# The first batch's slot pairs in three stages set apart in program order, and the filter's sign put in once

## The chip, the cores and the metric

The kernel runs on one core of one Trainium2 chip. A time is that of one execution in microseconds of device time; kernels are compared by the median of their runs. The profile is of one such execution.

## What is computed

Eight sequences of 3008 tokens with 256 channels go through a filter in the frequency domain and then through an MLP with an intermediate width of 2048. All inputs are float32 but for the MLP's weights, which arrive as float64.

```python
X = np.fft.rfft(x, axis=1)                    # x: 8 x 3008 x 256
Y = X * (filt_r + 1j * filt_i)[None]          # 1505 frequencies x 256
x = np.fft.irfft(Y, n=3008, axis=1).reshape(8 * 3008, 256)
h = x @ w_in                                  # 256 x 2048
out = (h / (1 + np.exp(-1.702 * h))) @ w_out  # 2048 x 256
```

## The kernel before

The length 3008 is 64 x 47. A forward transform is a DFT over 64 (tiles `s1`), a DFT over 47 (`s2`), the product with the filter, and the two inverse DFTs (`i2`, then `i1`). Real input leaves 32 slots of 48 rows and 256 channels; a step handles two slots, called a **pair** here, so a batch has 16 pairs. In a tile of a pair, rows 0 to 47 hold the real part and rows 64 to 111 the imaginary part (112 partitions, the 16 between are zero).

The first batch (`first_fft`) has nothing to run beside. Its six input tiles are multiplied by `t1_0` (L331) and copied to `a_t` (L334). Then for each pair g: TensorE (PE) transposes four 128x96 blocks (L342, tile `z`), ScalarE (ACT) copies them to SBUF (L344, `zs`), PE does the filter's DFT (L348, `s2`, printed as `s`), `product` multiplies by the filter on VectorE (DVE, L365 and L366) and GpSimd (POOL, L367), PE does the inverse DFT of the product (L354, `i2`, printed as `i`), and ACT copies the result into `b_t` (L355).

`product` is a complex multiplication. Some slots stand for the conjugate of a stored frequency, so the imaginary part of the filter has a sign of its own for each row and slot, in the table `sign`. Before, DVE put it in as a per-row scalar, in four operations of 48 rows x 256 channels for each pair, in every batch (L365).

Filter values are loaded by SyncE's DMA queue (SP) in two transfers of 192 KB for a pair, one for rows 0 to 47 and one for rows 64 to 111. In the first batch eight buffers `f_s` (made of `f_buf`, `f_y` and `f_o`) rotate, and loads run six pairs ahead.

The MLP's weights arrive as 64-bit values and are turned into pairs of float32 parts by ACT, DVE and POOL (`weights`, `weight`, L219 to L236). The generator `weights` has 20 steps: steps 0 to 3 only load a weight, step 4 loads the fifth and starts four conversions, and each later step starts one and finishes one. `run(w_parts, n)` runs n steps. After the first batch comes `mlp` for 48 tiles of up to 512 tokens (L515 to L529), and between its matmuls the transforms of later batches (`fft`) are spread; these use the same `product`, with `f_buf` loaded anew for each pair (L413).

The order of the instructions on an engine is set by a scheduler from the program's order. Instructions given to `keep_in_program_order` keep their order among themselves: among them are the loads of SP in the first part (`load_in`) and the first four ACT operations of `weight` (L219). Each engine, and the DMA queue of SP, takes its instructions in that order, so one that waits holds all behind it.

Of the kernel before, what the change touches and what calls it, by code (L numbers as in the profile page):

```python
# [9 lines left out]
F32 = mybir.dt.float32  # L10
# [19 lines left out]
def _tables():  # L30
# [65 lines left out]
    d_0[:96] = de[rows, 0:2]  # L96
    e_0 = de[:, 2:4, rows].reshape(P, 2, 2, 2, NH).transpose(0, 1, 4, 3, 2)
    sign = np.zeros((P, NS))
    sign[0:48], sign[64:Q] = _places()[3], -_places()[3]
    tabs = [t1_0, t1, t2, d_0, e_0, np.eye(P), sign, de]  # L100
    return np.concatenate([a.reshape(P, -1) for a in tabs], 1).astype(np.float32)

# [48 lines left out]
def tile_kernel(  # L151
# [145 lines left out]
    def first_fft():  # L297

        d_0 = table["d_0"].rearrange("p (m c) -> p m c", m=2)
        e_0 = table["e_0"].rearrange("p (m c) -> p m c", m=2)

        a_t = [const.tile([P, NS, 96], F32, tag=t, name=f"a_t{m}") for m, t in enumerate(("wi_1", "wo_1"))]
        f_s = [f_buf] + [sb.tile([Q, 4, 2, D], F32, tag="y", name=f"f_y{i}") for i in range(2)]
        f_s = [f[:, 2 * i : 2 * i + 2] for f in f_s for i in range(2)]
        f_s += [sb.tile([Q, 2, 2, D], F32, tag="out", name=f"f_o{i}") for i in range(2)]
        pin = tc.keep_in_program_order

        def load_f(g):  # L310
# [24 lines left out]
        yield
        for g in range(16):
            if 6 <= g + 6 < 16:
                load_f(g + 6)
            z_ps = bank(f"z_0_{g}")
            for u in range(2):  # L340
                for m in range(2):
                    nc.tensor.transpose(z_ps[:96, u, P * m : P * m + P], a_t[m][:, 2 * g + u], table["eye"])  # L342
            z = sb.tile([96, 2, D], F32, tag="half", name=f"zs_0_{g}", bufs=4)
            nc.scalar.copy(z, z_ps[:96])  # L344
            ps = bank(f"s2_0_{g}")
            ms = [(slice(0, 1), 1), (slice(1, 2), 0)] if g == 0 else [(slice(0, 2), 0)]
            for u, m in ms:
                nc.tensor.matmul(ps[:Q, u], d_0[:96, m], z[:, u], start=True, stop=True)  # L348
            u1 = c_buf[g % 3]
            product(g, ps, u1, f_s[g % 8])  # L350
            ps = bank(f"i2_0_{g}").rearrange("p a d -> p (a d)")[:, 0:384].rearrange("p (m u c) -> p m u c", m=2, u=2)
            for u in range(2):
                for m in range(2):
                    nc.tensor.matmul(ps[:, m, u], u1[:Q, u, P * m : P * m + P], e_0[:Q, int(g + u == 0)], start=True, stop=True)  # L354
            nc.scalar.copy(b_t[:, :, :, 2 * g : 2 * g + 2], ps.rearrange("p m u c -> p m c u"))  # L355
            yield

    def product(i, xs, u1, fr):

        u2 = u_buf[i % 2]  # L360
        f_r, f_i = fr[:, :, 0, :], fr[:, :, 1, :]
        for u in range(2):
            for h, o in ((slice(0, 48), slice(64, Q)), (slice(64, Q), slice(0, 48))):
                sg = sign[h, 2 * i + u : 2 * i + u + 1]
                nc.vector.scalar_tensor_tensor(u2[o, u], xs[h, u], sg, f_i[h, u], ALU.mult, ALU.mult)  # L365
        nc.vector.tensor_tensor(u1, xs[:Q], f_r, ALU.mult)  # L366
        nc.gpsimd.tensor_tensor(u1, u1, u2, ALU.add)  # L367

# [7 lines left out]
    def fft(b):  # L376
# [33 lines left out]

        def load_f(i):
            for k in range(2):
                load_in(f_buf[64 * k : 64 * k + 48, 2 * (i % 2) : 2 * (i % 2) + 2], filt[:, 2 * i : 2 * i + 2])  # L413

        def second(i, m, src, name):

# [212 lines left out]
```

## Time and profile before

| | |
|---|---|
| median of 3 runs | 2533.18 us (2532.65 to 2534.22) |
| profiled execution | 2531.02 us, of which its span is 2529.2 us |
| mean granted clock of PE | 0.974 |
| busy: PE, DVE, ACT, POOL | 2441.0, 1601.1, 1301.9, 831.3 us |

The span is the time from the first to the last instruction of the profile. In a row of the timeline stand the start, the busy time, the engine, line and operation, the output and input tiles, the shape, and in brackets the idle time before it and what ended that. In a row of groups stand the busy time, the mean of one in ns, and the idle time ahead of the group with what ended it. In a row of waits: who waited, for whom, us in total, how many times, and the longest.

### The profile page before, as it was taken

Reading aid. Unit: us, or ns where it says so; the run is one execution under the profiler, and the core shown is the slowest. Engines: PE = TensorE matmul, PEld = TensorE weight load, DVE = VectorE, ACT = ScalarE, POOL = GpSimd, SP = SyncE. Lnnn points to the kernel's source line nnn. Section 1 sums busy time; section 2 is a strip of 40 time slices with the busy share of each in tenths; the row PEclk is TensorE's granted clock in tenths of the full one; section 3 lists DMA queues with packets and bytes.
Section 4 is the critical chain, followed back from the end, with each engine's and each line's share of the span. In section 5 each row is a group of like instructions: output and inputs, shape, how many; then the busy total and the mean of one; then the engine's idle time right before and its main releaser. Section 6 shows DMA issues by size and latency. Waiting matters only on the chain.

```text
span 2529.2 us, 31965 instructions
## 1 busy us (share of the span) xinstructions
PE 2441.0 (97%) x11082; PEld 2005.1 (79%) x11082; DVE 1601.1 (63%) x2423; ACT 1301.9 (51%) x2409; POOL 831.3 (33%) x714
## 2 busy tenths in 40 slices
PE   7779999999999999999999999999999999999999
PEld 5457877887778888988877888888878888898887
DVE  4495788468845887378843887358863788432322
ACT  1265555555545555555554555555555565444443
POOL 2263454235422443244421454134432344100000
PEclk6589999999999999999999999999999999999999
DMA  6133543554445443454334343453434443300000
GB/s 180 44 100 108 117 110 85 133 133 111 107 113 137 102 103 92 133 121 98 92 104 123 97 103 81 127 129 96 110 84 134 102 105 93 72 15 9 17 9 17
DMA packets 139906, 243.48 MB, mean 96 GB/s; under 512 B 15328, under 2 KB 80992, under 8 KB 139744
## 3 DMA queue, kind: packets, MB, share of 16 engines
q1 hardware_dynamic: 61504, 130.58, 18.5%
q10 hardware_dynamic: 53152, 66.80, 10.0%
q0 software_dynamic: 25088, 44.05, 8.9%
q8 instruction: 88, 1.44, 0.2%
q14 instruction: 74, 0.61, 0.1%
HBM read 150.67 MB, written 90.70 MB: 95 GB/s over the span
## 4 chain that ended last, share of the span: by engine, by line
PE 73%; DMA 4%; DVE 3%; issue 1%; ACT 1%; SPq 0%; POOL 0%; ACTq 0%; POOLq 0%; DVEq 0%
PE o L529 32%; PE h L515 32%; PE i L486 3%; DMA br<-b_d 2%; PE s L423 2%; PE i L423 1%; DVE u_buf L365 1%; PE s L270 1%; PE s L269 1%; PE s L271 1%; DVE c_buf L374 1%; DVE gl L521 1%; DMA x<-in_x_dram 1%; DMA b_d<-b 1%; DMA zy<-a_d 1%
## 5 line engine op out<-in xcount | busy, mean ns | idle before, releaser
L515 PE MATMUL h<-y,wi 128*128 128x512 f32 (+1 forms) x4608 | 1173.8, 388 | 4.2 <-POOL wi L236 2.1
L521 DVE TENSOR_TENSOR gl<-g,gh 128x512 fp32r<-128x512 f32 (+1 forms) x768 | 650.0, 849 | 692.8 <-ACT gh L520 615.7
L515 PEld LDWEIGHTS h<-y,wi 128*128 128x128 f32 x4608 | 864.3, 189 | 178.4 <-POOL wi L236 3.3
L519 ACT ACTIVATE g<-h 128x512 f32<-128x512 f32 (+1 forms) x768 | 452.6, 589 | 917.7 <-PE h L515 802.8
L529 PE MATMUL o<-gh,wo 128*128 128x512 f32 (+1 forms) x3072 | 833.3, 390 | 15.6 <-ACT gh L520 11.6
L529 PEld LDWEIGHTS o<-gh,wo 128*128 128x128 f32 x3072 | 570.6, 189 | 137.4 <-ACT gh L520 18.3
L529 PE MATMUL o<-gl,wo 128*128 128x512 f32 (+1 forms) x1536 | 480.8, 389 | 11.7 <-DVE gl L521 11.4
L520 ACT ACTIVATE gh<-h 128x512 fp32r<-128x512 f32 (+1 forms) x768 | 448.4, 585 | 58.6 <-PE o L529 48.3
L438 POOL TENSOR_TENSOR zy<-c_buf,zy 48x512 fp32r<-48x512 f32 x224 | 335.4, 1497 | 93.2 <-DVE zy L437 81.9
L367 POOL TENSOR_TENSOR c_buf<-c_buf,u_buf 112x512 f32<-112x512 f32 x128 | 192.4, 1503 | 517.5 <-DVE c_buf L366 517.2
L529 PEld LDWEIGHTS o<-gl,wo 128*128 128x128 f32 x1536 | 284.6, 188 | 75.0 <-DVE gl L521 21.2
L387 POOL TENSOR_TENSOR xl<-x,xh 128x512 fp32r<-128x512 f32 x84 | 111.3, 1338 | 411.5 <-ACT xh L386 377.8
L365 DVE SCALAR_TENSOR_TENSOR u_buf<-c_buf,tab,f_buf 48x256 f32<-48x256 f32 x448 | 225.4, 542 | 6.6
L406 POOL DMA_DIRECT2D zy<-a_d x224 | 128.2, 575 | 285.9 <-PE s L423 102.4
L374 DVE TENSOR_TENSOR c_buf<-s,c_buf 48x512 f32<-48x512 f32 x224 | 154.2, 688 | 22.7 <-ACT c_buf L373 16.7
L374 DVE TENSOR_TENSOR b<-i,b 48x512 f32<-48x512 f32 x224 | 154.1, 688 | 8.8 <-ACT b L373 2.5
L373 ACT COPY c_buf<-s 48x512 f32<-48x512 f32 x224 | 130.1, 581 | 23.1 <-PE s L423 12.4
L373 ACT COPY b<-i 48x512 f32<-48x512 f32 x224 | 130.1, 581 | 16.6 <-DVE b L374 4.9
L437 DVE CAST zy<-c_buf 48x512 fp32r<-48x512 f32 x224 | 95.6, 427 | 56.9 <-POOL c_buf L367 52.9
L486 PEld LDWEIGHTS i<-tab,br 128*128 128x128 f32 x736 | 100.5, 195 | 26.8 <-issue 9.4
L486 PE MATMUL i<-tab,br 128*128 128x128 f32 x736 | 104.7, 280 | 13.6 <-DMA br<-b_d 9.6
L497 POOL CAST y<-carry 128x128 fp32r<-128x128 f32 x8 | 2.8, 375 | 261.0 <-PE h L515 260.8
(81 smaller groups left out, 1238.0 us busy)
## 6 DMA issues: line engine op xcount, KB each, us to landing
f_buf<-in_filt_dram SPq DMA_DIRECT2D x232, 192.0 KB, 3.2
zy<-a_d POOLq DMA_DIRECT2D x224, 192.0 KB, 3.6
x<-in_x_dram SPq DMA_DIRECT2D x48, 512.0 KB, 4.8
out_dram<-out SPq DMA_DIRECT2D x44, 512.0 KB, 3.4
a_d<-ah ACTq DMA_DIRECT2D x84, 256.0 KB, 3.5
a_d<-al ACTq DMA_DIRECT2D x84, 256.0 KB, 3.8
b_d<-b ACTq DMA_DIRECT2D x112, 192.0 KB, 2.6
br<-b_d SPq DMA_DIRECT2D x84, 256.0 KB, 4.6
```

The source lines that it names most:

```text
L365: nc.vector.scalar_tensor_tensor(u2[o, u], xs[h, u], sg, f_i[h, u], ALU.mult, ALU.mult)
L367: nc.gpsimd.tensor_tensor(u1, u1, u2, ALU.add)
L373: nc.scalar.copy(dst[h], ps[k][o])
L374: nc.vector.tensor_tensor(dst[h], ps[k][h], dst[h], ALU.add)
L406: nc.gpsimd.dma_start(zy[0][64 * k : 64 * k + 48, i % 2].rearrange("p k s d -> p k (s d)"), src.rearrange("n k s d -> n k (s d)"),)
L438: nc.gpsimd.tensor_tensor(y[o, k], u1[h], y[h, k].bitcast(F32), ALU.subtract)
L486: nc.tensor.matmul(ps[:, P * i : P * i + P], br[m][:, i], t2_sb, start=True, stop=True)
L515: nc.tensor.matmul(ps[:, :w], wi_sb[half][:, wk, kc, c], y[:, yk, kc, :w], start=n == 0, stop=n == 5)
L519: nc.scalar.activation(g[:, :w], ps[:, :w], AF.Gelu_apprx_sigmoid)
L520: nc.scalar.activation(gh[:, :w], ps[:, :w], AF.Gelu_apprx_sigmoid)
L521: nc.vector.tensor_tensor(gl[:, :w], g[:, :w], gh[:, :w].bitcast(F32), ALU.subtract)
L529: nc.tensor.matmul(pos[m][:, :w], wo[:, wk, P * m : P * m + P], gp[gk][:, :w], start=fc == 0 and n == 0, stop=fc == NFC - 1 and n == 2,)
```

## The change

1. The loop over the pairs of the first batch is cut into three functions. `turned(g)` is the transposes and their copy, `filtered(g)` the filter's DFT and the product, `inverse(g)` the inverse DFT and its copy. Step i of 19 runs `turned(i)`, `filtered(i - 1)` and `inverse(i - 3)`.
2. The sign is multiplied into the imaginary part of the filter by ACT, in two operations of 112x256 for each pair of the first batch, in `turned`. The signed rows 0 to 47 are stored to a DRAM buffer `fs` (192 KB for a pair, on SP's queue), and later batches load their filter from `fs`. The table `sign` now has the same sign in both halves.
3. `product` has two operations of 48x512 in place of four of 48x256: one with -1.0 as scalar, one plain multiplication.
4. Filter loads in the first batch run five steps ahead in place of six pairs.
5. The first eight steps of `weights` run after steps 2, 3, 5, 8, 13, 15, 17 and 19 of the first batch; before, four ran after steps 2, 5, 8 and 11 and four after the last pair.

```diff
-    sign[0:48], sign[64:Q] = _places()[3], -_places()[3]
+    sign[0:48] = sign[64:Q] = _places()[3]
...
+    fs = dram1.tile([48, NS, 2, D], F32, name="fs")
...
-        for g in range(16):
-            if 6 <= g + 6 < 16:
-                load_f(g + 6)
-            z_ps = bank(f"z_0_{g}")
+        def turned(g):
+            ps = bank(f"z_0_{g}")
...
+            zs[g] = sb.tile([96, 2, D], F32, tag="half", name=f"zs_0_{g}", bufs=4)
+            nc.scalar.copy(zs[g], ps[:96])
+            f = f_s[g % 8]
+            for u in range(2):
+                nc.scalar.activation(f[:, u, 1], f[:, u, 1], AF.Copy, scale=sign[:Q, 2 * g + u : 2 * g + u + 1])
+            load_in(fs[:, 2 * g : 2 * g + 2], f[0:48])
+
+        def filtered(g):
+            z = zs.pop(g)
...
+            product(g, ps, c_buf[g % 3], f_s[g % 8])
+
+        def inverse(g):
...
+        for i in range(19):
+            if 6 <= i + 5 < 16:
+                load_f(i + 5)
+            if i < 16:
+                turned(i)
+            if 1 <= i < 17:
+                filtered(i - 1)
+            if i >= 3:
+                inverse(i - 3)
             yield
...
-        for u in range(2):
-            for h, o in ((slice(0, 48), slice(64, Q)), (slice(64, Q), slice(0, 48))):
-                sg = sign[h, 2 * i + u : 2 * i + u + 1]
-                nc.vector.scalar_tensor_tensor(u2[o, u], xs[h, u], sg, f_i[h, u], ALU.mult, ALU.mult)
+        nc.vector.scalar_tensor_tensor(u2[0:48], xs[64:Q], -1.0, f_i[64:Q], ALU.mult, ALU.mult)
+        nc.vector.tensor_tensor(u2[64:Q], xs[0:48], f_i[0:48], ALU.mult)
...
-                load_in(f_buf[64 * k : 64 * k + 48, 2 * (i % 2) : 2 * (i % 2) + 2], filt[:, 2 * i : 2 * i + 2])
+                load_in(f_buf[64 * k : 64 * k + 48, 2 * (i % 2) : 2 * (i % 2) + 2], fs[:, 2 * i : 2 * i + 2])
...
-        if i in (2, 5, 8, 11):
+        if i in (2, 3, 5, 8, 13, 15, 17, 19):
             run(w_parts, 1)
-    run(w_parts, 4)
```

On the engines the order comes out as follows. PE, in the middle of the first batch, before (`z_5` is the transposed tile of pair 5, `s_0_4` the filter's DFT of pair 4, `i_0_3` the inverse of pair 3; the last number is the buffer's):

```order
L348 MATMUL s_0_4_303<-zs_4_301,tab 112x512
L354 MATMUL i_0_3_288<-tab,c_buf_78 128x96 x4
L342 MATMUL z_5_321<-tab,a_t_85 96x128
L342 MATMUL z_5_321<-tab,a_t_86 96x128
...
L354 MATMUL i_0_4_311<-tab,c_buf_79 128x96 x4
L348 MATMUL s_0_5_328<-zs_5_326,tab 112x512
```

Between the DFT of pair 4 and its inverse stood one inverse and one set of transposes. PE at the same place of the changed kernel:

```order
L366 MATMUL i_0_3_343<-tab,c_buf_79 128x96 x4
L359 MATMUL s_0_6_361<-zs_6_332,tab 112x512
L346 MATMUL z_8_377<-tab,a_t_86 96x128
L346 MATMUL z_8_377<-tab,a_t_87 96x128
...
L366 MATMUL i_0_4_367<-tab,c_buf_80 128x96 x4
L359 MATMUL s_0_7_387<-zs_7_356,tab 112x512
```

The transposes now run two pairs ahead of the DFT, and the DFT two to three pairs ahead of the inverse. ACT at the start of the pairs, before, from the fifth copy to `a_t` on:

```order
L334 COPY a_t_85<-s_0_4_0_175 128x128x4
L334 COPY a_t_85<-s_0_5_0_187 128x128x4
L344 COPY zs_0_206<-z_0_201 96x512
L344 COPY zs_1_230<-z_1_225 96x512
L355 COPY b_t<-i_0_0_217 128x192x2
L344 COPY zs_2_255<-z_2_250 96x512
```

ACT at the same place now; the rows of L351 are the sign operations on the filter's buffers, two for each pair:

```order
L351 ACTIVATE f_buf<-f_buf,tab 112x256
L337 COPY a_t_86<-s_0_4_0_176 128x128x4
L351 ACTIVATE f_buf<-f_buf,tab 112x256 x3
L337 COPY a_t_86<-s_0_5_0_188 128x128x4
L351 ACTIVATE f_y_88<-f_y_88,tab 112x256 x4
L348 COPY zs_0_205<-z_0_200 96x512
L348 COPY zs_1_217<-z_1_212 96x512
L351 ACTIVATE f_y_89<-f_y_89,tab 112x256 x2
L348 COPY zs_2_238<-z_2_233 96x512
```

The signs of pairs 0 to 3 now stand ahead of the first copy of transposes. On SP's queue, the transfers that follow the first six pairs' loads now:

```order
L180 DMA fs<-f_buf 48x1024
L180 DMA f_o_90<-in_filt_dram 48x1024 x2
L180 DMA fs<-f_buf 48x1024
L180 DMA w_229<-in_w_in_dram 128x512
L180 DMA f_o_91<-in_filt_dram 48x1024 x2
L180 DMA fs<-f_y_88 48x1024
L180 DMA w_249<-in_w_out_dram 128x512
L180 DMA f_buf<-in_filt_dram 48x1024 x2
```

A store to `fs` now stands ahead of the loads of each further pair, with weight loads (`w`) among them. DVE at the end of the pairs, where the first operations on weights (L227 to L229, writing `w_tu`) now stand among the products:

```order
L388 TENSOR_TENSOR c_buf_79<-s_0_12_519,f_y_89 112x512
L227 TENSOR_SCALAR w_tu<-w_tu 128x512 x4
L386 SCALAR_TENSOR_TENSOR u_buf_83<-s_0_13_541,f_y_89 48x512
L387 TENSOR_TENSOR u_buf_83<-s_0_13_541,f_y_89 48x512
L388 TENSOR_TENSOR c_buf_80<-s_0_13_541,f_y_89 112x512
L228 TENSOR_SCALAR w_tu<-w_tu 128x512 x4
...
L229 TENSOR_SCALAR w_tu<-w_tu 128x512 x3
L386 SCALAR_TENSOR_TENSOR u_buf_83<-s_0_15_587,f_o_91 48x512
```

Eleven such operations moved ahead of the last product; before, all stood behind it.

More of the change, by code (lines that the diff above doesn't have):

```diff
@@ L335, in first_fft @@
         yield
-        for g in range(16):
-            if 6 <= g + 6 < 16:
-                load_f(g + 6)
-            z_ps = bank(f"z_0_{g}")
+        zs = {}
+        def turned(g):
+            ps = bank(f"z_0_{g}")
             for u in range(2):
                 for m in range(2):
-                    nc.tensor.transpose(z_ps[:96, u, P * m : P * m + P], a_t[m][:, 2 * g + u], table["eye"])
-            z = sb.tile([96, 2, D], F32, tag="half", name=f"zs_0_{g}", bufs=4)
-            nc.scalar.copy(z, z_ps[:96])
+                    nc.tensor.transpose(ps[:96, u, P * m : P * m + P], a_t[m][:, 2 * g + u], table["eye"])
+            zs[g] = sb.tile([96, 2, D], F32, tag="half", name=f"zs_0_{g}", bufs=4)
[6 more added lines that the diff above has]
+            z = zs.pop(g)
             ps = bank(f"s2_0_{g}")
@@ L348, in first_fft @@
                 nc.tensor.matmul(ps[:Q, u], d_0[:96, m], z[:, u], start=True, stop=True)
-            u1 = c_buf[g % 3]
-            product(g, ps, u1, f_s[g % 8])
+            product(g, ps, c_buf[g % 3], f_s[g % 8])
+        def inverse(g):
             ps = bank(f"i2_0_{g}").rearrange("p a d -> p (a d)")[:, 0:384].rearrange("p (m u c) -> p m u c", m=2, u=2)
@@ L353, in first_fft @@
                 for m in range(2):
-                    nc.tensor.matmul(ps[:, m, u], u1[:Q, u, P * m : P * m + P], e_0[:Q, int(g + u == 0)], start=True, stop=True)
+                    nc.tensor.matmul(
+                        ps[:, m, u], c_buf[g % 3][:Q, u, P * m : P * m + P], e_0[:Q, int(g + u == 0)], start=True, stop=True
+                    )
             nc.scalar.copy(b_t[:, :, :, 2 * g : 2 * g + 2], ps.rearrange("p m u c -> p m c u"))
+        for i in range(19):
[7 more added lines that the diff above has]
+                inverse(i - 3)
             yield
```

## The prediction

> **What bounds the kernel now.** First the page, for the shares; then the busy times cut into three stages.
>
> ```profile
> span 2529.2 us, 31965 instructions
> PE 2441.0 (97%) x11082; PEld 2005.1 (79%) x11082; DVE 1601.1 (63%) x2423; ACT 1301.9 (51%) x2409; POOL 831.3 (33%) x714
> PEclk6589999999999999999999999999999999999999
> 20.00:117.00 97.00, 72.94 (x222) 45.40 (x220) 41.96 (x80) 16.49 (x32) 20.19 (x16) 0.54 0.32 86
> 117.00:212.00 95.00, 70.37 (x265) 52.07 (x266) 85.90 (x110) 55.65 (x102) 62.52 (x40) 0.82 0.27 78
> 212.00:2529.00 2317.00, 2283.60 (x10497) 1893.86 (x10495) 1466.33 (x2224) 1224.92 (x2270) 742.97 (x648) 1.00 0.38 96
> ```
>
> The columns of a window are its length, then busy time of PE, PEld, DVE, ACT, POOL, the granted clock, the DMA share and GB/s. After 212 us PE works 98.6% of the time at clock 1.00: that part is bound by matmuls, and the change touches none of them. Ahead of it lie two stages that PE does not fill usefully. From 117 to 212 DVE is the bound (85.9 of 95 us; it converts the weights). From 20 to 117, the sixteen steps of two slots ("pairs" here), no engine is full: PE shows 75% at a granted clock of 0.54, so it is both waiting and slow. The waits of PE ahead of 210 us and one cycle of its timeline say why.
>
> ```profile
> PE i L354 <- POOL c_buf L367: 18.6, 15, 4.3
> PE s L348 <- ACT zs L344: 5.4, 8, 0.7
> 45.78 2.02 PE L354 MATMUL i<-tab,c_buf 112*128 112x96 f32 x8 [0.67 <-POOL c_buf L367]
> 47.59 1.06 PE L342 MATMUL z<-tab,a_t 128*96 128x128 f32 x4
> 49.41 2.02 PE L354 MATMUL i<-tab,c_buf 112*128 112x96 f32 x8 [0.76 <-POOL c_buf L367]
> 51.23 1.94 PE L348 MATMUL s<-zs,tab 96*112 96x512 f32 x2
> 52.96 1.06 PE L342 MATMUL z<-tab,a_t 128*96 128x128 f32 x4
> 54.75 2.05 PE L348 MATMUL s<-zs,tab 96*112 96x512 f32 x2 [0.73 <-ACT zs L344]
> 21.94 2.03 DVE L365 SCALAR_TENSOR_TENSOR u_buf<-s,tab,f_buf 48x256 f32<-48x256 f32 x4 [2.47 <-DMA f_y<-in_filt_dram]
> 45.21 2.02 DVE L365 SCALAR_TENSOR_TENSOR u_buf<-s,tab,f_y 48x256 f32<-48x256 f32 x4 [0.88 <-issue]
> 56.89 2.03 DVE L365 SCALAR_TENSOR_TENSOR u_buf<-s,tab,f_o 48x256 f32<-48x256 f32 x4 [0.87 <-issue]
> 110.79 1.98 DVE L365 SCALAR_TENSOR_TENSOR u_buf<-s,tab,f_o 48x256 f32<-48x256 f32 x4 [5.31 <-issue]
> 116.99 0.48 ACT L355 COPY b_t<-i 128x384 f32<-128x384 f32 x1 [7.51 <-PE i L354]
> 118.07 0.43 DVE L224 TENSOR_SCALAR w_tu<-w_tu 128x512 f32<-128x512 f32 x1 [4.60 <-ACT w_tu L219]
> ```
>
> Two pairs take 56.89 - 45.21 = 11.7 us on DVE, so one takes 5.84 us. In each cycle PE stops for the product (0.7 us, on POOL) and for the copy of the transposes (0.7 us, on ACT), because the chain transposes, copy, filter DFT, product, inverse is run nearly one pair at a time. These stops are short, and still the clock stays low, which is the larger cost. The clock in one-microsecond windows shows it:
>
> ```profile
> 89.78 1.11 PE L348 MATMUL s<-zs,tab 96*112 96x512 f32 x2 [0.73 <-ACT zs L344]
> 88.00:89.00 1.00, 1.00 (x5) 0.61 (x3) 0.64 (x2) 0.00 (x0) 0.00 (x0) 0.56 0.00 0
> 92.54 2.02 PE L354 MATMUL i<-tab,c_buf 112*128 112x96 f32 x8 [1.65 <-POOL c_buf L367]
> 90.00:91.00 1.00, 0.89 (x2) 0.05 (x1) 0.97 (x2) 0.00 (x0) 0.00 (x0) 1.00 0.00 0
> 93.00:94.00 1.00, 1.00 (x7) 1.00 (x7) 0.83 (x2) 0.00 (x0) 0.00 (x0) 0.50 0.00 0
> 160.00:180.00 20.00, 13.86 (x55) 9.68 (x54) 19.76 (x25) 11.73 (x22) 13.39 (x9) 0.99 0.36 106
> ```
>
> Once, near 88.9 us, the clock rises to 1.00 and the same filter DFT takes 1.11 us, not 2.05; at 93 us, after waits of 0.7 and 1.65 us, it has fallen. From 160 to 180 us, though, PE is busy 69% and keeps 0.99. So a nearly gapless stretch raises it, and 70% work then holds it.
>
> **The change, part by part.** The durations:
>
> ```profile
> L344 ACT COPY zs<-z 96x512 f32<-96x512 f32 x16 | 9.2, 581 | 19.5 <-PE z L342 19.5
> L355 ACT COPY b_t<-i 128x384 f32<-128x384 f32 x16 | 7.8, 485 | 62.5 <-PE i L354 62.5
> L293 ACT CAST de_sb<-tab 48x192 fp32r<-48x192 f32 x2 | 0.7, 344 | 0.0
> L219 ACT ACTIVATE w_tu<-w 128x512 f32<-128x512 f32 x16 | 10.6, 680 | 2.0 <-POOL wi L236 1.0 <-POOL wo L236 0.9
> L366 DVE TENSOR_TENSOR c_buf<-s,f_y 112x512 f32<-112x512 f32 x8 | 5.5, 692 | 0.2
> L367 POOL TENSOR_TENSOR c_buf<-c_buf,u_buf 112x512 f32<-112x512 f32 x16 | 20.2, 1262 | 88.6 <-DVE c_buf L366 88.6
> L374 DVE TENSOR_TENSOR c_buf<-s,c_buf 48x512 f32<-48x512 f32 x224 | 154.2, 688 | 22.7 <-ACT c_buf L373 16.7
> 15.00:20.00 5.00, 4.44 (x40) 4.19 (x39) 2.07 (x3) 1.17 (x2) 0.00 (x0) 1.00 1.04 249
> f_y<-in_filt_dram SPq DMA_DIRECT2D x16, 192.0 KB, 4.8
> ```
>
> *The three stages.* PE's row now has the transposes of pair g+1 or g+2 and the inverse of an earlier pair between a filter DFT and its own inverse, so neither stop need recur; a pair then costs what its busiest engine needs.
> PE at half clock, start to start: inverse 51.23 - 49.41 = 1.82, filter DFT 52.96 - 51.23 = 1.73, transposes about 1.0 (the 1.06 of the row less its overlap), together 4.5 us. At full clock, scaled by 1.11 / 2.05 = 0.54: 2.45 us.
> DVE: three operations of 0.69 = 2.07 us, where it spent 2.02 + 0.69 = 2.71. POOL: 1.26 as before.
> ACT: 0.58 + 0.485 and two sign operations of 112x256. That shape has no row; it lies between 0.344 (48x192) and 0.680 (128x512, also from SBUF), and by length it is nearest to the first: 0.344 + 64 x 0.336 / 320 = 0.41. So ACT needs 1.07 + 0.82 = 1.9 us (2.4 at the upper bound), below PE.
> DMA: a pair loads 2 x 192 KB and now stores 192 KB. At the 249 GB/s that the filter loads get when the share is 1.04, 590 kB are 2.4 us; the four weight loads (512 KB each) that stand among the sixteen pairs add 2.1 MB / 16 / 249 = 0.5. Together 2.9 us per pair, if SP never holds a transfer back.
> So a pair costs 2.9 us where PE's clock is full (DMA ends last), 4.5 us where it is half. At half clock PE has no reason to stop, and the stretch of 88.9 us shows that such a run raises the clock; at full clock PE works 2.45 of 2.9 = 84%, above the 69% that held it. It will cool where loads come late, at the start above all. I take two thirds at full clock: (2 x 2.9 + 4.5) / 3 = 3.4 us. Bounds 2.9 and 4.5.
> *The start.*
>
> ```profile
> 0.00:20.00 20.00, 14.04 (x102) 13.79 (x103) 6.94 (x10) 4.79 (x7) 5.59 (x10) 1.00 0.93 291
> ```
>
> ACT's row puts the signs of pairs 0 to 3 ahead of the first copy of transposes, and a sign waits for its filter load. By 20 us 291 x 20 = 5.82 MB have come; six x tiles of 512 KB and 704 KB of tables are 3.87 of them, so 1.95 MB, five pairs of 393 kB, are filter, and pair 3's bytes are there near 18.5 us. With its two or four last signs (0.8 to 1.6 us) and the landing, the first copy starts between 20 and 22 us; the filter DFT that the product of pair 0 waits for was already at its end at 21.94. I let pair 0 reach DVE 1 us later, at 23 us (bounds 22 and 26).
> *The sum of the stage.* 23 + 15 x 3.4 = 74.0 for the start of the last product. Between pairs 12 and 15 DVE also does eleven of the weights' first operations (0.42 each, 4.6 us, against a slack of 3 x (3.4 - 2.07) = 4.0): + 0.6. The product ends at 76.7, where it ended at 110.79 + 1.98 + 0.69 = 113.5. Its tail (POOL, inverse, copy) is the same: **gain 36.8 us**.
> *The weights moved forward.* The first conversions stood behind the last copy; DVE idled 4.60 us ahead of 118.07 us. Those 4.6 us and the eleven operations (4.6 us) leave the stage that DVE bounds: 9.2 at most. The next DVE operations need POOL and ACT in turn, as they did before, so part of the idle time returns: **gain 6 us** (2 to 9).
> *SP's queue.* Sixteen stores stand between loads, and each waits for the sign of its pair; what queues behind is the filter load of a pair four or more later and the weight loads. A load needs 4.8 us to land, one and a half pairs: covered by that lead. If the lead goes, this is the slower rival below.
> *Later batches.* Two operations of 48x512 replace four of 48x256:
>
> ```profile
> L365 DVE SCALAR_TENSOR_TENSOR u_buf<-c_buf,tab,f_buf 48x256 f32<-48x256 f32 x448 | 225.4, 542 | 6.6
> PE i L486 <- DMA br<-b_d: 9.6, 12, 2.1
> PE o L529 <- DVE gl L521: 4.4, 7, 1.2
> PE i L423 <- DVE b L374: 1.1, 2, 0.9
> ```
>
> Four at 0.542 are 2.17 us, two at 0.688 (the 48x512 row above) 1.38: DVE is relieved of 112 x 0.79 = 88 us. PE is the bound there, and waits for DVE only 5.5 us in all, with 9.6 us for loads that follow DVE's results. The loads from the new buffer have the old size. Bounds: 15 gained, or 4 lost (two of the longest waits of 2.1) since the queues are ordered anew; **gain 3 us**.
> *Sum.* 36.8 + 6 + 3 = 46 us. The profiled execution took 2531.0 us (1.8 around its span), 2.2 below the median of 2533.2. So 2485 against it, **2487 us** against the median.
>
> **Rivals.**
> *Full clock throughout.* Pairs at 2.9 us: 15 x 0.5 = 7.5 us better, less 1 us as DVE's slack for the weights shrinks: 2480. For it speaks 160 to 180 us; against it the fall by 93 us, after waits of no more than 1.65 us, and the loads' late start. The Trainium skill, "TensorE: Matmul & The Clock Gate", Part 1, has the gate close only after about one idle window of 3.4 us; by that rule this rival would be the forecast, but the trace disagrees: it had closed by 93 us, with PE at work in 0.89 of the microsecond from 90.
> *Half clock throughout.* 15 x 1.1 = 16.5 us worse: 2504. For it: the stretch from 49.41 to 54.02 us was gapless for 4.6 us and the next filter DFT still took 2.05. Against it: 88.9 us. The same page, Part 4, says that transposes do not count as busy for the gate; by it only 3.55 of each 4.5 us would count, and this rival would be the forecast. No run here shows the transposes alone.
> *Slower: the signs hold ACT.* If each sign waited for a load issued only behind the store of the pair before, a pair would take 4.8 (landing) + 0.8 (sign) + about 1.3 (store and load issue) = 6.9 us: 15 x (6.9 - 5.84) = 16, plus the 1 us of the start, less 9 gained behind it: 2541. It decides from about 6.4 us a pair on. Against it: loads are issued six pairs ahead at the start and the sixteen slots of time behind them need only 590 kB each.
>
> **Chances.** Mixed clock (2478 to 2499) 0.61; full clock 0.16; half clock 0.16; held by the signs 0.07, of which 0.04 ends over 0.2% slower, 0.02 within 0.2%, and 0.01 faster. 0.2%, 5 us, is about what a measurement of this kernel can tell from no change. So faster 0.94, same 0.02, slower 0.04. The range takes in both clock rivals with their bounds (weights 2 to 9, later batches -4 to 15): 2470 to 2508.
>
> **What would show it.** Filter products on DVE 3 to 4 us apart, the last ending near 77 us; PE's clock in 20 to 80 us between 0.6 and 0.9; no PE wait for POOL in the steady pairs; the weights' stage shorter by about 6 us; PE's busy time after it unchanged within 5 us. I am wrong if ACT waits for filter loads pair after pair, if PE runs gapless at 0.50, or if the weights' stage grows by what the first one lost.

## The result, and the profile after

The changed kernel takes 2466.38 us (median; 2465.0 to 2467.85), the kernel before, run beside it on the same chip, 2532.91 us: ratio 0.9739, interval 0.9722 to 0.9756. That is 66.5 us less, where 46 were forecast. The profiled execution took 2467.57 us, 63.5 us less than that of before.

The head of the page, with the granted clock in 40 slices:

```profile
span 2465.7 us, 31786 instructions
PEclk9799999999999999999999999999999999999999
```

The slices of before began with 6 5 8; now only the second is below 9. The windows of the changed kernel (length, then busy time of PE, PEld, DVE, ACT, POOL, the clock, the DMA share, GB/s), the last one from tile 0's output copy to the end:

```profile
20.00:40.00 20.00, 16.80 (x99) 11.56 (x98) 15.52 (x23) 12.90 (x30) 8.81 (x7) 1.00 1.03 306
40.00:60.00 20.00, 16.28 (x98) 11.44 (x96) 18.16 (x30) 13.52 (x31) 10.67 (x8) 1.00 0.90 276
60.00:80.00 20.00, 10.83 (x44) 8.66 (x45) 16.12 (x21) 8.98 (x16) 17.73 (x11) 0.54 0.32 103
155.80:2465.70 2309.90, 2277.75 (x10498) 1892.99 (x10496) 1415.48 (x2001) 1225.04 (x2271) 730.41 (x648) 1.00 0.38 96
```

While the pairs run the clock is 1.00, not a mixture, and the transfers carry 306 and 276 GB/s, above the 249 that the prediction took for their ceiling. The clock falls to half between 61 and 62 us, when the last pairs run. The timeline of the changed kernel shows what sets the pace and where it breaks:

```profile
23.31 0.69 DVE L386 SCALAR_TENSOR_TENSOR u_buf<-s,f_buf 48x512 f32<-48x512 f32 x1 [4.07 <-PE s L359]
41.11 0.69 DVE L386 SCALAR_TENSOR_TENSOR u_buf<-s,f_buf 48x512 f32<-48x512 f32 x1
43.29 0.69 DVE L386 SCALAR_TENSOR_TENSOR u_buf<-s,f_buf 48x512 f32<-48x512 f32 x1
41.29 1.03 PE L366 MATMUL i<-tab,c_buf 112*128 112x96 f32 x8
42.16 1.04 PE L359 MATMUL s<-zs,tab 96*112 96x512 f32 x2
43.03 0.60 PE L346 MATMUL z<-tab,a_t 128*96 128x128 f32 x4
43.47 1.03 PE L366 MATMUL i<-tab,c_buf 112*128 112x96 f32 x8
52.98 2.50 DVE L227 TENSOR_SCALAR w_tu<-w_tu 128x512 f32<-128x512 f32 x4
62.10 0.69 DVE L386 SCALAR_TENSOR_TENSOR u_buf<-s,f_o 48x512 f32<-48x512 f32 x1
63.54 0.69 DVE L388 TENSOR_TENSOR c_buf<-s,f_o 112x512 f32<-112x512 f32 x1
60.12 1.13 PE L366 MATMUL i<-tab,c_buf 112*128 112x96 f32 x8 [2.69 <-POOL c_buf L389]
63.25 2.02 PE L366 MATMUL i<-tab,c_buf 112*128 112x96 f32 x8 [2.00 <-POOL c_buf L389]
64.31 3.78 POOL L389 TENSOR_TENSOR c_buf<-c_buf,u_buf 112x512 f32<-112x512 f32 x1 [1.12 <-DVE c_buf L388]
68.15 2.02 PE L366 MATMUL i<-tab,c_buf 112*128 112x96 f32 x8 [2.88 <-POOL c_buf L389]
70.20 0.49 ACT L369 COPY b_t<-i 128x384 f32<-128x384 f32 x1 [0.23 <-PE i L366]
155.75 0.69 DVE L564 COPY out<-o 128x512 f32<-128x512 f32 x1 [2.42 <-PE o L551]
```

In the steady part products start 43.29 - 41.11 = 2.18 us apart, with no idle time ahead of them: DVE's three operations of 0.69 us, back to back, with small gaps between them. PE is level with it here: from inverse to inverse it takes 43.47 - 41.29 = 2.18 us without a gap, 0.87 for each DFT and 0.44 for the transposes. The last pairs are slower: weights' operations stand between the products on DVE, PE waits 2 to 3 us for POOL each time, the clock falls (an inverse takes 2.02 us at 63.25, 1.13 at 60.12), and POOL's addition takes 3.78 us, where its mean in the kernel before was 1.26.

The same two landmarks, last copy to `b_t` and tile 0's output copy, cut each profile into three pieces. Before, the copy to `b_t` stands at 116.99 (shown in the prediction), and the rest is:

```profile
211.21 0.69 DVE L542 COPY out<-o 128x512 f32<-128x512 f32 x1 [2.20 <-PE o L529]
211.20:2529.20 2318.00, 2284.40 (x10500) 1894.51 (x10498) 1467.12 (x2225) 1225.72 (x2271) 743.17 (x649) 1.00 0.38 96
```

All kernels of this study, in us, each from its one profile. The middle piece is from the last copy to tile 0, the later part from there to the end of the span. Runs of one kernel lie up to 8.6 us apart (e4b_fill1, 2520.33 to 2528.91, of which the profiled one took 2528.32), so a difference of a few us between two rows, in the later part above all, can be that of two executions:

| kernel | last copy to `b_t` | middle piece | later part | span |
|---|---|---|---|---|
| before | 116.99 | 94.2 | 2318.0 | 2529.2 |
| after | 70.20 | 85.6 | 2310.0 | 2465.7 |
| e1_order | 71.19 | 92.3 | 2323.6 | 2487.1 |
| e2_sign | 110.34 | 97.7 | 2312.6 | 2520.7 |
| e3_wlate | 63.42 | 93.1 | 2305.6 | 2462.1 |
| e4_filler | 103.48 | 93.3 | 2319.6 | 2516.4 |
| e4b_fill1 | 97.76 | 97.9 | 2330.8 | 2526.5 |
| e5_dve | 75.72 | 92.9 | 2311.0 | 2479.6 |
| e6_nostore | 63.99 | 93.1 | 2303.4 | 2460.4 |
| e7_lo_dve | 62.12 | 82.0 | 2310.8 | 2454.9 |
| e9_later4 | 61.53 | 93.1 | 2314.3 | 2468.9 |
| e10_fwd_dve | 74.78 | 72.1 | 2310.3 | 2457.2 |

### The profile page after: what moved, and what is told of

Read it like the earlier page. It is cut to its first block, busy times and chain, and to the rows that moved or that the text cites. A ratio compares the mean times of both kernels' runs of the same rounds, so it can differ in the third digit from the quotient of the medians.

```text
span 2465.7 us, 31786 instructions
## 1 busy us (share of the span) xinstructions
PE 2398.9 (97%) x11082; PEld 1986.8 (81%) x11082; DVE 1538.4 (62%) x2167; ACT 1313.0 (53%) x2441; POOL 824.3 (33%) x714
## 4 chain that ended last, share of the span: by engine, by line
PE 78%; DVE 7%; DMA 5%; issue 2%; ACT 2%; POOL 1%; SPq 1%; ACTq 1%; POOLq 0%; DVEq 0%
PE o L551 35%; PE h L537 35%; PE i L508 3%; DVE gl L543 2%; DMA br<-b_d 2%; PE s L445 2%; PE i L445 2%; DMA x<-in_x_dram 1%; DVE c_buf L396 1%; DMA zy<-a_d 1%; DMA b_d<-b 1%; POOL c_buf L389 1%; PE s L272 1%; PE s L274 1%; PE s L273 1%
## 5 line engine op out<-in xcount | busy, mean ns | idle before, releaser
L543 DVE TENSOR_TENSOR gl<-g,gh 128x512 fp32r<-128x512 f32 (+1 forms) x768 | 657.2, 858 | 737.7 <-ACT gh L542 653.3
L389 POOL TENSOR_TENSOR c_buf<-c_buf,u_buf 112x512 f32<-112x512 f32 x128 | 185.2, 1447 | 457.9 <-DVE c_buf L388 456.8
L459 DVE CAST zy<-c_buf 48x512 fp32r<-48x512 f32 x224 | 94.2, 421 | 51.9 <-POOL c_buf L389 47.9
L387 DVE TENSOR_TENSOR u_buf<-c_buf,f_buf 48x512 f32<-48x512 f32 x112 | 87.6, 782 | 3.6
```

The costliest lines, as they stand in the source:

```text
L543: nc.vector.tensor_tensor(gl[:, :w], g[:, :w], gh[:, :w].bitcast(F32), ALU.subtract)
```

## The experiments

Each was timed beside the kernel before on the same chip; e1 to e4 share one set of runs of it (2531.95 us), e4b to e7 another (2531.44), e9 and e10 a third (2531.25).

### e1_order: the order alone

The changed kernel with the old product, the old table and no signs or store; the weights' steps are where they stood before. Filter loads run five steps ahead, as in the changed kernel.

```diff
-            f = f_s[g % 8]
-            for u in range(2):
-                nc.scalar.activation(f[:, u, 1], f[:, u, 1], AF.Copy, scale=sign[:Q, 2 * g + u : 2 * g + u + 1])
-            load_in(fs[:, 2 * g : 2 * g + 2], f[0:48])
...
-        nc.vector.scalar_tensor_tensor(u2[0:48], xs[64:Q], -1.0, f_i[64:Q], ALU.mult, ALU.mult)
-        nc.vector.tensor_tensor(u2[64:Q], xs[0:48], f_i[0:48], ALU.mult)
+        for u in range(2):
+            for h, o in ((slice(0, 48), slice(64, Q)), (slice(64, Q), slice(0, 48))):
+                sg = sign[h, 2 * i + u : 2 * i + u + 1]
+                nc.vector.scalar_tensor_tensor(u2[o, u], xs[h, u], sg, f_i[h, u], ALU.mult, ALU.mult)
```

> The three-stage order alone: sign put in by VectorE as before (four operations of 48x256 a pair), no signed store, later batches as before, weights' steps at their old places. Theory 1 (the order keeps TensorE's clock up, and a pair then costs what VectorE needs): VectorE needs 2.03 + 0.69 = 2.72 us a pair, so the last product starts near 23 + 15 x 2.75 = 64 us (110.8 before, 62.1 with the whole change), clock 1.00 from 20 to 60 us, and the run takes 2533 - 46 = 2487 us. Theory 2 (the shorter product did it, the order alone leaves the clock at half): 4.5 us a pair, last product at 91 us, 2513 us.

Measured 2487.65 us, ratio 0.9825 (0.981 to 0.9839). Its timeline and a window:

```profile
64.98 2.03 DVE L384 SCALAR_TENSOR_TENSOR u_buf<-s,tab,f_o 48x256 f32<-48x256 f32 x4
71.19 0.48 ACT L364 COPY b_t<-i 128x384 f32<-128x384 f32 x1 [2.23 <-PE i L361]
40.00:60.00 20.00, 17.29 (x104) 12.13 (x103) 18.84 (x37) 7.99 (x15) 9.29 (x8) 1.00 0.71 202
```

The order alone takes the last copy from 116.99 to 71.19 us, 45.8 us, and raises the clock: to 0.83 from 20 to 40 us and 1.00 from 40 to 60, where it was 0.60 and 0.50 before. The pairs are then (64.98 - 22.39) / 15 = 2.84 us apart (22.39 is the first product's start), close to the old product's 2.03 + 0.69 = 2.72 us on DVE. So the order hands the stage to DVE, in which 18.84 of 20 us are busy.

### e2_sign: the sign alone

The kernel before with the new table, the signs on ACT, the store, the short product, and `fs` for later batches; the loop over the pairs as it was.

```diff
             nc.scalar.copy(z, z_ps[:96])
+            f = f_s[g % 8]
+            for u in range(2):
+                nc.scalar.activation(f[:, u, 1], f[:, u, 1], AF.Copy, scale=sign[:Q, 2 * g + u : 2 * g + u + 1])
+            load_in(fs[:, 2 * g : 2 * g + 2], f[0:48])
...
-        for u in range(2):
-            for h, o in ((slice(0, 48), slice(64, Q)), (slice(64, Q), slice(0, 48))):
-                sg = sign[h, 2 * i + u : 2 * i + u + 1]
-                nc.vector.scalar_tensor_tensor(u2[o, u], xs[h, u], sg, f_i[h, u], ALU.mult, ALU.mult)
+        nc.vector.scalar_tensor_tensor(u2[0:48], xs[64:Q], -1.0, f_i[64:Q], ALU.mult, ALU.mult)
+        nc.vector.tensor_tensor(u2[64:Q], xs[0:48], f_i[0:48], ALU.mult)
```

> The sign on ScalarE, the signed store and the shorter product, with the old order of the pairs and the weights' steps at their old places. Theory 1: the chain of two pairs loses one product's 0.65 us in 11.7, so the first stage gains some 5 us, the clock stays near 0.55, and the later batches gain the 8 us that they gained with the whole change: 2520 us. Theory 2 (the shorter product is what counts): the first stage gains 30 us or more: 2495 us or less.

Measured 2522.43 us, ratio 0.9961 (0.9947 to 0.9976). The last copy and a window:

```profile
110.34 0.48 ACT L360 COPY b_t<-i 128x384 f32<-128x384 f32 x1 [6.92 <-PE i L359]
60.00:80.00 20.00, 15.77 (x48) 9.68 (x47) 8.28 (x12) 5.64 (x12) 5.05 (x4) 0.50 0.78 209
```

In the old order the shorter product is worth 6.7 us in the stage: the clock is 0.50 in this window and no higher than 0.67 in the other three of 20 us up to 100, and DVE, busy 8.28 of 20 us, is far from the bound. Order and sign together (e3, next) gain 69.4 us, order alone 44.3 and sign alone 9.5, so together they bring 15.6 us more than apart. The stage accounts for little of that: the sign takes 6.7 us off its end in the old order and 71.19 - 63.42 = 7.8 in the new. A pair does fall from 2.84 to 2.23 us there, which is 9 us over 15 pairs, but e3's first product starts 2.9 us later than e1's. Most lies in the later part, where the sign takes 18.0 us in the new order (2323.6 - 2305.6) and 5.4 in the old; why it takes so much more there was not tested.

### e3_wlate: the weights' steps where they were

```diff
-        if i in (2, 3, 5, 8, 13, 15, 17, 19):
+        if i in (2, 5, 8, 11):
             run(w_parts, 1)
+    run(w_parts, 4)
```

> The whole change but for the weights' steps, which stand at their old places: eleven conversion operations go back behind the last product. Theory A (the prediction's: moving them is worth some 6 us, since VectorE idles behind the last product otherwise): 2466 + 6 = 2472 us, with the last product near 58 us and an idle time of VectorE of 4 to 5 us behind it. Theory B (VectorE bounds both stages, so it only moves work): 2466 us, within 2.

Measured 2462.56 us (2459.42 to 2464.21), ratio 0.9724 (0.971 to 0.9739); the changed kernel's interval, 0.9722 to 0.9756, overlaps it. Its first and last product, the landmarks and DVE's first conversion between them:

```profile
25.26 0.69 DVE L386 SCALAR_TENSOR_TENSOR u_buf<-s,f_buf 48x512 f32<-48x512 f32 x1 [6.12 <-PE s L359]
58.72 0.69 DVE L386 SCALAR_TENSOR_TENSOR u_buf<-s,f_o 48x512 f32<-48x512 f32 x1
63.42 0.48 ACT L369 COPY b_t<-i 128x384 f32<-128x384 f32 x1 [1.61 <-PE i L366]
64.50 0.43 DVE L227 TENSOR_SCALAR w_tu<-w_tu 128x512 f32<-128x512 f32 x1 [3.65 <-ACT w_tu L222]
156.51 0.69 DVE L564 COPY out<-o 128x512 f32<-128x512 f32 x1 [1.97 <-PE o L551]
```

Without the steps forward the pairs end 6.8 us earlier and the middle piece is 7.5 us longer; tile 0 is written within 0.8 us of the same time. DVE idles 3.65 us ahead of the first conversion again, and tile 0 comes no later for it. What the steps forward do is a shift between two stages that DVE bounds. The time, 3.8 us below the changed kernel's, lies outside the 2 us that theory B allowed; the later part in the table is 4.4 us shorter here, and why was not tested.

### e4_filler and e4b_fill1: the clock alone

The kernel before, with PE's order in the first batch held as it was and three matmuls of 128x384 (in e4b one) ahead of each inverse, into the PSUM bank that the inverse then overwrites. PE gets work that is of no use, to see whether it keeps the clock up. No run held the order without a filler.

```diff
+            for _ in range(3):
+                nc.tensor.matmul(flat[:, 0:384], table["eye"], tab[:, 0:384], start=True, stop=True)
             for u in range(2):
                 for m in range(2):
                     nc.tensor.matmul(
```

> The kernel before with TensorE's order in the pairs pinned as it was, and three matmuls of 384 columns that nobody needs put ahead of each inverse (overwritten by it), so that TensorE works on while it waits for the product. Theory 1 (half of the loss in the old stage was the low clock): clock near 1.00 from 30 to 100 us; a cycle of two pairs falls from 11.7 to some 8.3 us (filter DFT, transposes and inverse at full clock: 2.2 + 5.2 + 0.9), 25 us gained: 2508 us. Rival (the clock is a by-product of waits that the chain of product and copies sets): cycle of 11 us or more, 2528 us or more; if the clock does not rise, the extra matmuls cost about 1.2 us a pair, 2550 us.

> The kernel before with its order pinned and one extra matmul of 384 columns ahead of each inverse in place of three. With three, a cycle of two pairs took 9.6 us, and the inverse followed the extra ones with a wait of 0.1 to 0.5 us, so they lay partly on the path. Theory (clock and chain): one of them (0.65 us) lies within the wait; if the clock still rises, the cycle is 8.3 to 8.8 us, last product near 90 us, 2512 us. Rival (the chain of copies and product sets the cycle): 9.4 us as with three, 2519 us. If one does not raise the clock: 11.7 to 12 us a cycle, 2533 us.

Three fillers: 2519.82 us, ratio 0.9954 (0.9937 to 0.997). One: 2525.52 us, ratio 0.9975 (0.9965 to 0.9985). The windows and the start of an inverse in the two kernels, e4_filler first:

```profile
60.00:80.00 20.00, 17.94 (x82) 11.18 (x81) 11.31 (x23) 4.29 (x8) 5.07 (x4) 1.00 0.46 138
63.27 1.13 PE L365 MATMUL i<-tab,c_buf 112*128 112x96 f32 x8 [0.51 <-POOL c_buf L385]
72.82 1.13 PE L365 MATMUL i<-tab,c_buf 112*128 112x96 f32 x8
```

```profile
40.00:60.00 20.00, 13.25 (x66) 7.79 (x64) 11.82 (x24) 4.28 (x8) 6.01 (x5) 1.00 0.50 134
69.45 1.13 PE L365 MATMUL i<-tab,c_buf 112*128 112x96 f32 x8 [1.38 <-POOL c_buf L385]
78.55 1.13 PE L365 MATMUL i<-tab,c_buf 112*128 112x96 f32 x8 [1.38 <-POOL c_buf L385]
```

With one filler the clock holds 1.00 from 40 us on while PE is busy 13.25 of 20 us, 66%. Two pairs then take 78.55 - 69.45 = 9.1 us, where they took 11.7, and the last copy (97.76 us) comes 19.2 us earlier than before. With three fillers the clock is as full, but the fillers lie on the path: 72.82 - 63.27 = 9.55 us for two pairs. So a full clock without the new order is worth under half of the 45.8 us that the order brings; with the order PE's waits for POOL and ACT in each pair go as well. Both expectations were missed: the cycles lie between those of the two theories of each, and both kernels took longer than the clock theory had it. In e4b most of the 19.2 us is lost again behind the stage (97.9 and 2330.8 us in the table). The clock accounts for most of the longer later part: summed over windows of 10 us, the time that a clock below full takes away, (1 - clock) x 10 us, is about 14.2 us there against 3.4 before, 10.8 of the 12.8 us of difference. What lowered the clock there was not tested.

### e5_dve: one more DVE operation in each pair of the first batch

e3 with an operation whose result is overwritten, ahead of the product:

```diff
+            nc.vector.tensor_tensor(u_buf[g % 2][64:Q], ps[0:48], f_s[g % 8][0:48, :, 1, :], ALU.mult)
             product(g, ps, c_buf[g % 3], f_s[g % 8])
```

> As the kernel with the weights' steps at their old places (2462.6 us), with one more VectorE operation of 48x512 in each product of the first batch (it writes rows that the next one writes over). Theory 1 (VectorE paces the pairs at 2.2 us): the pairs go 2.9 us apart, the last product starts 15 x 0.72 = 11 us later, 2473 us. Rival 1 (the loads pace the pairs, VectorE is hidden): up to 3 us, 2463 to 2466. Rival 2 (TensorE at full clock paces them with 2.3 us a pair): up to 9 us less the slack, 2471, and TensorE shows no more waits for the product than before.

Measured 2478.89 us, ratio 0.9788 (0.9771 to 0.9804). Two added operations in its timeline, a stop of PE, and the last copy:

```profile
40.79 0.68 DVE L360 TENSOR_TENSOR u_buf<-s,f_y 48x512 f32<-48x512 f32 x1
43.66 0.68 DVE L360 TENSOR_TENSOR u_buf<-s,f_o 48x512 f32<-48x512 f32 x1
32.27 2.05 PE L359 MATMUL s<-zs,tab 96*112 96x512 f32 x2 [3.43 <-ACT zs L348]
75.72 0.48 ACT L370 COPY b_t<-i 128x384 f32<-128x384 f32 x1 [2.32 <-PE i L367]
```

A pair takes 43.66 - 40.79 = 2.87 us, 0.69 more than the 2.18 of the changed kernel: what is added to DVE is added to the pair. The stage ends 12.3 us later than in e3, 16 x 0.69 = 11.0 and a little for the one stop of 3.43 us, after which the filter's DFT takes 2.05 us (half clock). ACT's copy came late there because ACT had waited 3.30 us for a filter load. The whole took 5.9 us more than the 2473 of theory 1; 5.4 of them are in the later part (2311.0 against 2305.6).

### e6_nostore: the transfers relieved

e3 without the store of the signed filter; later batches load `filt`, so this kernel leaves out their signs.

```diff
-            load_in(fs[:, 2 * g : 2 * g + 2], f[0:48])
...
-                load_in(f_buf[64 * k : 64 * k + 48, 2 * (i % 2) : 2 * (i % 2) + 2], fs[:, 2 * i : 2 * i + 2])
+                load_in(f_buf[64 * k : 64 * k + 48, 2 * (i % 2) : 2 * (i % 2) + 2], filt[:, 2 * i : 2 * i + 2])
```

> As the kernel with the weights' steps at their old places (2462.6 us), without the sixteen signed stores; later batches load the unsigned filter (the sign is left out there). Theory 1 (VectorE paces the pairs, the transfers run just beside it): 1 to 3 us less from the fewer waits of ScalarE for loads, 2460 to 2462. Rival (transfers pace the pairs: the DMA share was 0.9 to 1.0 from 20 to 60 us): a pair moves 393 kB in place of 590, some 0.6 us less a pair, so pairs at VectorE's 2.17 without a gap and 4 to 6 us gained, 2457 to 2459.

Measured 2464.49 us, ratio 0.9735 (0.9721 to 0.975), no faster than e3; both theories had expected a gain.

```profile
63.99 0.48 ACT L367 COPY b_t<-i 128x384 f32<-128x384 f32 x1 [1.61 <-PE i L364]
40.00:60.00 20.00, 19.42 (x125) 14.64 (x124) 18.55 (x27) 12.07 (x26) 10.76 (x9) 1.00 0.63 172
```

The DMA share falls to 0.63 in this window, products stay 2.18 us apart there (41.38 and 43.56 us), and the last copy does not move (63.99 against 63.42). So from 40 us on the transfers are not what the pairs wait for. From 20 to 40 us the share is 1.03 without the stores too, and there loads did stop PE once: ACT waited 2.15 us for `f_o` and 0.82 for `f_buf`, PE then 2.15 us for ACT's copy, and from 31.67 to 39.21 us two pairs took 7.5 us in place of 4.4.

### e9_later4: the old count of DVE operations in later batches

e3, in which only the later batches have four operations of 48x256 (with constant scalars) for the product's first half:

```diff
+        if xs is u1:
+            for u in range(2):
+                for h, o, sg in ((slice(0, 48), slice(64, Q), 1.0), (slice(64, Q), slice(0, 48), -1.0)):
+                    nc.vector.scalar_tensor_tensor(u2[o, u], xs[h, u], sg, f_i[h, u], ALU.mult, ALU.mult)
+        else:
+            nc.vector.scalar_tensor_tensor(u2[0:48], xs[64:Q], -1.0, f_i[64:Q], ALU.mult, ALU.mult)
+            nc.vector.tensor_tensor(u2[64:Q], xs[0:48], f_i[0:48], ALU.mult)
-        nc.vector.scalar_tensor_tensor(u2[0:48], xs[64:Q], -1.0, f_i[64:Q], ALU.mult, ALU.mult)
-        nc.vector.tensor_tensor(u2[64:Q], xs[0:48], f_i[0:48], ALU.mult)
```

> e3_wlate with one thing undone in later batches only: their product again has four DVE operations of 48x256 (constant scalars) in place of two of 48x512; the first batch keeps the short product, the signs and the store. Theory 1 (the later batches gain because PE waits less often for DVE's results once DVE is relieved of some 88 us there): the part from tile 0's output copy to the end comes back to the 2318 to 2331 us of the kernels with the old product, PE's waits there for DVE and ACT (gl, gh) rise from about 5 us to about 10 us, and the whole takes 2471 to 2480 us with the stage of the pairs unchanged (last copy to b_t near 63.5 us). Theory 2 (the later part differs for other reasons, such as the loads from the stored copy or a schedule that happens to fit): it stays at 2303 to 2313 us, and the whole at 2460 to 2466 us.

Measured 2473.72 us (2470.88 to 2475.09), ratio 0.977 (0.9756 to 0.9785), above e3's interval. Its later part and PE's waits there for the tiles that ACT and DVE make for the second MLP matmul (`gh`, `gl`), then the two rows of e3, from which it differs by this one thing:

```profile
154.60:2468.90 2314.30, 2277.72 (x10500) 1894.51 (x10498) 1433.10 (x2225) 1227.06 (x2272) 731.13 (x648) 1.00 0.38 96
PE o L556 <- DVE gl L548: 5.6, 6, 2.1
PE o L556 <- ACT gh L547: 5.1, 6, 1.7
```

```profile
PE o L551 <- DVE gl L543: 3.8, 7, 1.1
PE o L551 <- ACT gh L542: 1.7, 4, 0.9
```

The later part grows from 2305.6 to 2314.3 us, 8.7 of the 12.4 that separate e3 from before, and these waits from 5.5 us (in e3) to 10.7. The shorter product in later batches is thus worth some 9 to 11 us. The first theory's number for the whole held, its number for the part (2318 or more) did not; the other 3.7 us lie within the spread of the table (2303.4 to 2312.6 for kernels with the short product). The count came back here, but only part of DVE's time: an operation with a constant scalar takes 479 ns, where one with the per-row scalar took 542, and DVE's busy time in the later part is 1433.1 us, against 1417.6 in e3 and 1467.1 before. Whether that makes up the 3.7 us was not tested.

### e7_lo_dve and e10_fwd_dve: the weights' conversion taken from POOL

e3 (e7) and the changed kernel (e10) with both POOL operations of `weight` on DVE:

```diff
-            nc.gpsimd.tensor_tensor(w, u.bitcast(F32), w, ALU.add)
+            nc.vector.tensor_tensor(w, u.bitcast(F32), w, ALU.add)
...
-        nc.gpsimd.tensor_tensor(lo, w, hi.bitcast(F32), ALU.subtract)
+        nc.vector.tensor_tensor(lo, w, hi.bitcast(F32), ALU.subtract)
```

> As the kernel with the weights' steps at their old places (2462.6 us), with the 32 additions and subtractions of the weights' conversion on VectorE in place of GpSimd. Theory L (the weights' stage of 93 us is long because operations of VectorE and GpSimd hold each other up: 0.42 us ones take 1.5, 0.68 us ones 1.8, and GpSimd's 1.26 us ones 1.7): VectorE then needs its operations at their undisturbed times, some 60 us, plus 32 x 0.68 = 22: 82 us, 10 us gained, 2452 us. Rival (VectorE was simply full with its 83 us): 83 + 22 = 105 us, 2475 us.

> e7_lo_dve (both GpSimd operations of the weights' conversion on DVE, 2457.6 us) with the weights' first eight steps forward among the pairs, as the change has them. If moving them forward only moves DVE's work from one stage that it bounds to another: last copy to b_t about 7 us or more later (70 to 75 us), the weights' stage shorter by the same, total within 4 us of e7 (2455 to 2462 us). If the forward steps fill idle time of DVE (the prediction's step): 2449 to 2453 us. If they cost more than they bring, since the cycle of the pairs is broken and PE's clock falls, and DVE now has more operations there: 2462 to 2470 us.

Measured 2457.57 us, ratio 0.9706 (0.9691 to 0.972), and 2457.31 us, ratio 0.9704 (0.9688 to 0.972). A landmark and a group of DVE in e7_lo_dve, then a landmark of e10_fwd_dve; ahead of them the same group in e3, where POOL still had its part:

```profile
L227 DVE TENSOR_SCALAR w_tu<-w_tu 128x512 f32<-128x512 f32 x16 | 12.1, 757 | 3.7 <-ACT w_tu L222 3.7
```

```profile
144.15 0.69 DVE L564 COPY out<-o 128x512 f32<-128x512 f32 x1 [0.89 <-PE o L551]
L227 DVE TENSOR_SCALAR w_tu<-w_tu 128x512 f32<-128x512 f32 x16 | 6.7, 418 | 3.7 <-ACT w_tu L222 3.6
```

```profile
146.87 0.69 DVE L564 COPY out<-o 128x512 f32<-128x512 f32 x1 [1.59 <-PE o L551]
```

Both beat the changed kernel, and are the best versions here. The middle piece falls from 93.1 to 82.0 us, although DVE, its bound, got 32 operations more: each of its old ones became shorter. That is the 82 us that theory L had for this piece; the whole gained 5.0 us on e3 and not 10, since the later part was 5.1 us longer, within what single executions differ by. Between e7 and e10 the steps forward move 12.7 us into the pairs and take 9.9 out of the middle piece; the totals are the same. That repeats e3 against the changed kernel: the steps forward are worth nothing that can be measured.

## Why the prediction was wrong

It had the direction right, and that a pair would cost what its busiest engine needs once the stages are set apart. It had the wrong engine and the wrong clock, and missed its range by 3.6 us (2466.4, with 2470 as the lower end).

**The start: right.** The first product was put at 23 us and came at 23.31.

**The pace of a pair: the step that failed.** "I take two thirds at full clock: (2 x 2.9 + 4.5) / 3 = 3.4 us." Two terms in it were wrong. The clock was 1.00 for all but the last pairs (1.00 in the windows from 20 to 60 us), so the half-clock third, 15 x 0.5 = 7.5 us, did not occur. The other 10 us lie in the full-clock pair itself, put at 2.9 us. "DMA ends last", at 249 GB/s, took what the loads happened to carry in one window for what they can carry: 306 and 276 were seen, and e6 shows that less traffic gains nothing. DVE has no slack at 2.18 us, which e5 shows by adding to it, and e1 by DVE's longer product (2.84 us a pair). PE's gapless cycle is just as long, and no run took work from DVE alone to see whether PE would hold the pairs at 2.18. The prediction had DVE at 2.07 us, which leaves out the small gaps between operations, and PE at 2.45, since it scaled the distances from start to start by a ratio of busy times (0.54), where the distances halve (1.82 to 0.87 for the inverse at half and at full clock). Over 15 pairs with no weights between, e3's 58.72 - 25.26 = 33.5 us (starts of its last and first product) is 2.23 us each, against 3.4: 17.5 us of error.

**The weights between the products: mis-sized.** "+ 0.6" was 5.3: 62.10 - 23.31 = 38.8 us in the changed kernel, against e3's 33.5. The slack had been worked out for pairs of 3.4 us, and at 2.2 us DVE has none. This hid part of the first error: 74.6 + 0.3 - 17.5 + 4.7 = 62.1 us, the measured start of the last product. The tail was not "the same" either. From the product's end to the last copy it took 70.20 - 64.23 = 6.0 us, where it had taken 116.99 - 113.47 = 3.5, with POOL's addition at 3.78 us and PE at half clock.

**The weights moved forward: the number came out, the cause did not.** From the last product's end to tile 0 the time fell from 97.7 to 91.5 us, 6.2 where 6 were forecast. But e3 and e10 show that this is the other side of what the pairs lost, and no gain.

**Later batches: mis-sized.** 3 was taken, 8.0 measured (2318.0 - 2310.0), inside the bounds of -4 to 15. The relief of DVE was itself smaller than the 88 us taken: its busy time in the later part fell by 51.6 us (1467.1 to 1415.5); the two new operations take 711 and 782 ns there, where 688 was taken. The prediction priced it by the 5.5 us for which PE waits for DVE by name, yet waits put down to ACT (`gh`, 5.7 us before, 3.4 after) fell as well. e9 shows on e3 that the short product is worth 8.7 us there, as waits of PE. In the changed kernel itself the rows do not add up that way: all waits of PE in the later part fall by only 1.5 us (28.2 to 26.7) and its busy time by 6.6, so the cause of most of the 8.0 us stays open.

In sum the product's end gained 113.47 - 64.23 = 49.2 us where 36.8 were forecast, the middle 6.2 where 6, the later part 8.0 where 3: 63.5 us in the profiles.

**The rivals.** Full clock throughout was right about the clock up to the last pairs and still 14 us too slow, since it kept 2.9 us a pair. By the Trainium skill, "TensorE: Matmul & The Clock Gate", Part 1, the clock falls only after about one idle window of 3.4 us; the prediction set that rule aside because of a fall by 93 us, and the steady pairs went the rule's way. It does not cover the falls, though: ahead of three of them PE was at work in 33% to 46% of a stretch of 3.4 us (rows in the last section). Half clock throughout is refuted: transposes take 0.6 us of each pair, and the clock was full. The signs did not hold the pairs. ACT waited for filter loads 8.4 us in all from 24 to 64 us, in six waits: those on `f_y` are in the row below (us in all, times, longest), and those on the other buffers were 3.1 and 2.0 us. Their longest hold on PE in that stretch was 0.9 us; in e5 and e6 such waits stopped PE once, for 3.43 and 2.15 us. A pair's two sign operations took 0.91 us, where 0.82 was taken.

```profile
ACT f_y L351 <- DMA f_y<-in_filt_dram: 3.3, 2, 2.7
```

**What would show it.** The last product's end near 77 us: 64. Products 3 to 4 us apart: 2.18. PE's clock from 20 to 80 us between 0.6 and 0.9: 0.85, but by luck, as it was 1.00 up to 61 us and 0.5 behind the fall. No PE wait for POOL in the steady pairs: one of 0.5 us, then the two of 2.69 and 2.00 us once the weights came in between. PE's busy time after the stage the same within 5 us: 2284.4 before, 2277.8 after, so it fell by 6.6, outside the 5.

## What to carry to other kernels

When a serial chain is overlapped, work out each engine's time for a step and forecast the largest of them as the pace, with PE's time taken at full clock if little idle time is left; take a transfer for the bound only if its rate was seen under pressure. Then look at what else has been put on that engine: work moved from one stage to another that the same engine bounds gains nothing. Where operations on two engines slow each other, as those of DVE and POOL did here, moving all of them to one is worth a try, even to the busier one.

## What the runs showed of the hardware

**What holds the clock, and what closes it.** One filler a pair, with PE busy 66% in e4b (13.25 of 20 us) and waits up to 1.8 us, held 1.00. Three stretches of 3.4 us just ahead of a fall to half clock, of before, the changed kernel and e5_dve, and one of e4b at the end of its pairs (columns as above, PE's busy time second):

```profile
88.90:92.30 3.40, 1.27 (x3) 0.27 (x2) 3.21 (x7) 0.58 (x1) 1.08 (x1) 1.00 0.00 0
58.10:61.50 3.40, 1.13 (x8) 0.97 (x8) 3.34 (x8) 0.21 (x1) 2.25 (x2) 1.00 0.05 18
27.00:30.40 3.40, 1.57 (x12) 1.32 (x12) 3.24 (x6) 0.17 (x1) 1.47 (x2) 1.00 0.95 286
92.00:97.00 5.00, 1.42 (x6) 0.60 (x5) 2.62 (x5) 0.01 (x1) 1.26 (x1) 1.00 0.00 0
```

PE was at work in 37%, 33% and 46% of the first three stretches, and the clock fell at their ends. So a stretch of some 3.4 us that is only partly idle can close it. In e5 it fell 1.6 us into the wait of 3.43 us. In e4b, though, PE was busy 28% of 5 us, with one wait of 3.58 us, and the inverse behind that wait still took 1.13 us; the clock fell only between 97 and 98 us. So neither the busy share of a stretch nor the length of a wait settles it alone. What else does was not tried.

**DVE and POOL slow each other.** With POOL at work on the weights, DVE's operation of L227 took 757 ns (e3), without it 418 (e7). In the changed kernel POOL's addition in the product took 1.27 us in the steady pairs and 1.98 to 3.78 us in the last four, when weights' operations ran on DVE beside it. The Trainium skill, "SBUF — State Buffer", "Who interferes with whom", says that DVE and GpSimd share one pair of ports, which one instruction holds to its end; these numbers agree with it, though no run here looked at the ports alone.
